# RWKV-6 attention and a gated feed-forward on one core: token pairs for the first four blocks, and the whole order of work changed

## The chip, the cores and the metric

The kernel runs on one NeuronCore of a Trainium2 chip. The core has five engines with queues of their own: TensorE (PE; its weight loads are listed as PEld), VectorE (DVE), ScalarE (ACT), GpSimd (POOL) and SyncE (SP), which issues most of the DMAs. Each engine takes its instructions in the order in which they were written and waits where an operand is not there yet. Sixteen DMA engines move data between HBM and the on-chip memory SBUF; TensorE writes to eight PSUM banks. The metric is the device time of one launch in microseconds (us); less is better.

## The reference

Inputs are r, k, v, w of shape (4 batches, 8 heads, 768 tokens, 48), u of (8, 48), and the weights of a feed-forward layer. First a recurrence over tokens, for every batch and head:

```python
for t in range(S):
    cur = np.einsum('bhd,bhe->bhde', u[None] * kt, vt)
    y[:, :, t] = np.einsum('bhd,bhde->bhe', rt, state + cur)
    state = wt[:, :, :, None] * state + np.einsum('bhd,bhe->bhde', kt, vt)
```

Then x, the rows of y with the heads side by side (3072 rows of 384), goes through:

```python
rms = np.sqrt(np.mean(x * x, axis=-1, keepdims=True) + 1e-06)
xn = x / rms * rms_g
g = xn @ w_gate                      # 384 -> 1536
silu = g * (1.0 / (1.0 + np.exp(-g)))
return (silu * (xn @ w_val) @ w_out) # 1536 -> 384
```

## The kernel before

**Blocks.** The 768 tokens of a batch are six chunks of 128. A block n.j is chunk n of batch j, 24 in all; its tokens lie on the 128 partitions, its 8 x 48 = 384 values on the free axis. Inside a block the recurrence becomes products. `ln` takes the logarithm of w, `cs_mm` sums it over tokens on TensorE with a triangular mask, `exp_r` and `exp_k` give decay factors, `r_mul` and `k_mul` apply them to r and k in bf16. `rk_pe` transposes the two on TensorE and `rk_tr` copies the result to SBUF (for chunks 2 to 5 `rk_tr` is a DMA transpose on SP instead). `q_mm` makes the scores of the even heads and of the odd heads in two PSUM banks, `q_mask_e`, `q_copy_o` and `q_mask_o` mask them, and `y_mm` multiplies them with v (`cast_v`, bf16) and adds the older state's part. `st_mm` and `st_new` carry the state to the next chunk. The term with u is apart: `bonus_mul` (r times k times u) and `bonus_v` on GpSimd, `bonus_sum` on VectorE; `x_add` on VectorE adds it to y.

**Feed-forward.** `x_sq`, `x_rstd`, `xn_mul` normalise; `xn_pe` and `xn_out` transpose and apply the gain (the last two chunks use a DMA transpose `xn_tr` and `xn_gain` on GpSimd). Four blocks make a group of 512 columns. For each group there are 12 `gate_mm` and 12 `val_mm` (one bank each, L617 or L622), `silu` on ScalarE, `h_mul` on VectorE, and four output products `o_mm` (12 matmuls each, L660) with `o_out` and `out_dma`. The groups follow the chunks, but the first holds blocks 0.0, 0.1, 1.0 and 1.1, and the second 0.2, 0.3, 1.2 and 1.3.

**Pairs of w.** For chunks 0 and 1 (set `WIN`) w is loaded for both chunks at once, with two neighbouring tokens on a partition, so that a DMA packet holds 2 x 48 fp32 = 384 bytes; r, k and v, and w of the other chunks, come in packets of 192. `cs_mm` then needs two products for each of its sums (L404, L411) and mask `mw`; elsewhere (`ONE_SUM`) it needs one (L419), and `cs_add` on VectorE makes the second sum from the first.

**What sets the order.** A table `ORDER` of some 1,050 steps, written out by hand, is walked from top to bottom; each step appends its instructions to the engines it uses. So the table fixes the order on every engine, the loads on SP and the four loads of gate and value weights on GpSimd (`load_gv`, L351) included. A number after a colon asks for fillers ahead of a step: matmuls with zeros (L238, L240) that keep TensorE running. Sets such as `CAST_ACT` or `K_POOL` choose the engine of a step. PSUM banks rotate in rings: two "a", two "b", four "q". SBUF tiles rotate too: eight tiles each for r, k and v (`NIN`), six for the transposed r and k (`NRKT`).

Of the kernel before, what the change touches and what calls it, by code (L numbers as in the profile page):

```python
# [9 lines left out]
FP32 = mybir.dt.float32  # L10
BF16 = mybir.dt.bfloat16
# [14 lines left out]
load_r.0.0 load_w.0.0 u_mm.0.0 ln.0.0 load_v.0.0 load_k.0.0 cs_mm.0.0:2 load_r.1.0 load_w.0.1 u_out.0.0 load_k.1.0  # L26
load_k.0.1 load_w.0.3 load_v.0.1 exp_r.0.0 exp_k.0.0 r_mul.0.0 cast_v.0.0 load_r.0.1 bonus_mul.0.0 load_k.1.1
bonus_sum.0.0 bonus_v.0.0 k_mul.0.0 cs_mm.1.0 load_r.1.1 load_v.1.1 load_v.1.0 load_w.0.2 rk_pe.0.0:2 rk_tr.0.0
exp_r.1.0 w_tot.1.0 w_tot.0.0 st_mm.0.0 r_mul.1.0 st_new.0.0 q_mm.0.0:4 load_k.0.3 load_r.0.3 load_r.0.2 load_k.0.2
load_v.0.2 ln.0.1 q_mask_o.0.0 exp_k.1.0 cs_mm.0.1 exp_r.0.1 k_mul.1.0 exp_k.0.1 rk_pe.1.0 load_v.0.3 rk_tr.1.0  # L30
bonus_mul.1.0 q_mask_e.0.0 load_k.1.3 load_r.1.2 load_k.1.2 load_r.1.3 load_v.1.2 bonus_mul.0.1 load_w.2.1 load_w.2.0
load_v.1.3 load_w.2.3 q_mm.1.0:2 cs_mm.1.1 exp_r.1.1 exp_k.1.1 r_mul.0.1 k_mul.0.1 w_tot.0.1 q_mask_o.1.0
bonus_sum.1.0 load_gv.0.1 cast_v.0.1 load_r.2.0 bonus_sum.0.1 r_mul.1.1 load_w.2.2 rk_pe.0.1:2 ln.0.3 y_mm.0.0
rk_tr.0.1 st_mm.0.1:4 x_add.0.0 q_mask_e.1.0 st_new.0.1 cs_mm.0.3:3 bonus_v.0.1 cast_v.1.0 q_mm.0.1:1 y_mm.1.0
k_mul.1.1 bonus_v.1.0 cast_v.1.1 q_copy_o.0.1 x_sq.0.0 bonus_mul.1.1 load_r.2.1 x_add.1.0 exp_r.0.3 load_r.2.2
x_sq.1.0 load_r.2.3 load_k.2.0 q_mask_e.0.1 w_tot.1.1 rk_pe.1.1:1 rk_tr.1.1 q_mm.1.1:7 q_mask_o.1.1 load_gv.0.0
q_mask_o.0.1 y_mm.0.1:8 g_mm.0.0 bonus_sum.1.1 ln.0.2 x_rstd.1.0 xn_mul.1.0 x_rstd.0.0 xn_mul.0.0 exp_k.0.3
bonus_v.1.1 load_gv.1.0 q_mask_e.1.1 x_add.0.1 x_sq.0.1 x_rstd.0.1 y_mm.1.1 x_add.1.1 k_mul.0.3 xn_pe.1.0:2 xn_pe.0.0
cs_mm.0.2 g_out.0.0 xn_out.1.0 x_sq.1.1 xn_mul.0.1 xn_out.0.0 r_mul.0.3 st_mm.1.1:3 x_rstd.1.1 st_mm.1.0 xn_mul.1.1
# [90 lines left out]
def kernel(  # L130
# [130 lines left out]
    def load_w(n, j):  # L261
# [4 lines left out]
        else:  # L266
            if ("w", n, j) not in inp:
                inp["w", n, j - j % 2] = inp["w", n, j - j % 2 + 1] = pin.tile([128, 2 * DM], FP32, name="wt", bufs=NIN // 2)
# [445 lines left out]
```

## Time and profile before

| | |
|---|---|
| time, median of three runs | 204.7 us (204.5 to 206.58) |
| the profiled execution | 203.96 us, its span 202.2 us |
| granted TensorE clock | 0.998 |
| busy: TensorE, VectorE, ScalarE, GpSimd | 95%, 78%, 67%, 62% of the span |
| DMA packets | 121,567, of which 116,420 under 512 bytes |
| first feed-forward matmul, end of the last matmul | 30.21 us, 199.0 us |

The span runs from the first instruction to the last. A busy TensorE includes fillers, and the matmul ends are modelled, so starts are the surer number. In rows of groups the last figures are the busy time, the mean ns of one, and the idle time of the engine before them with what ended it; in rows in order of time the first two figures are start and duration, and a bracket gives the idle time before the instruction.

### The profile page before, as it was taken

The numbers are of one execution on the slowest core, as the hardware profiler recorded it, in microseconds if no ns is written. First come the engines' busy times: TensorE is split into PE (matmuls) and PEld (weight loads), VectorE is DVE, ScalarE is ACT, GpSimd is POOL, SyncE is SP. The second block draws the span as 40 slices with busy tenths as digits, with TensorE's granted clock in tenths as the row PEclk, the third lists the DMA queues.
The fourth block names the chain that finished last, engine by engine and source line by source line (L and its number), as shares of the span: only waits on it lengthen the run. The fifth ranks groups of instructions, "written<-read, shape, count | busy, mean of one in ns | idle before, by whom it ended". The sixth has DMA issues, their size and how long they took to land.

```text
span 202.2 us, 4604 instructions
## 1 busy us (share of the span) xinstructions
PE 191.3 (95%) x1677; PEld 121.9 (60%) x1694; DVE 157.5 (78%) x307; ACT 135.0 (67%) x278; POOL 124.4 (62%) x178
## 2 busy tenths in 40 slices
PE   1999799999999999999999998999999999999993
PEld 0566485565568998865556664656555555555562
DVE  6489789799989799997999998988989782225711
ACT  2637885779699657898678985899676683335310
POOL 6488959175769962689858556988699554200000
PEclk9999999999999999999999999999999999999999
DMA  6999999999999998989899999995464013030132
GB/s 144 231 234 207 212 208 202 195 179 208 206 184 225 160 212 191 210 185 188 199 176 215 237 188 203 183 190 108 134 179 104 0 23 99 0 117 0 63 115 99
DMA packets 121567, 32.42 MB, mean 160 GB/s; under 512 B 116420, under 2 KB 120392, under 8 KB 121544
## 3 DMA queue, kind: packets, MB, share of 16 engines
q1 hardware_dynamic: 119504, 28.58, 66.6%
q0 software_dynamic: 2032, 3.54, 9.9%
q8 instruction: 13, 0.21, 0.4%
q14 instruction: 10, 0.08, 0.1%
q10 hardware_dynamic: 8, 0.00, 0.0%
HBM read 25.96 MB, written 4.72 MB: 152 GB/s over the span
## 4 chain that ended last, share of the span: by engine, by line
PE 65%; ACT 3%; DMA 2%; DVE 2%; issue 1%; SPq 0%; DVEq 0%; ACTq 0%
PE ps_av L617 7%; PE ps_bu L617 7%; PE ps_au L617 7%; PE ps_bv L617 6%; PE ps_qx L660 6%; PE ps_qv L660 6%; PE ps_qu L660 5%; PE ps_qz L660 4%; PE ps_au L622 2%; PE ps_bu L622 2%; DMA rkT<-rk 2%; PE ps_av L622 2%; PE ps_bv L622 2%; ACT L249 1%; PE ps_au L419 1%; PE ps_qv L500 1%
## 5 line engine op out<-in xcount | busy, mean ns | idle before, releaser
L660 PEld LDWEIGHTS <-ht 128*128 128x128 bf16 x300 | 28.1, 98 | 17.5 <-DVE ht L646 1.0
L251 ACT ACTIVATE sg<-ps_av 128x512 bf16<-128x512 f32 x36 | 21.5, 597 | 22.8 <-PE ps_av L617 18.0
L646 DVE TENSOR_TENSOR ht<-ps_bv,sg 128x512 bf16<-128x512 f32 x29 | 19.9, 687 | 13.9 <-PE ps_bv L617 12.9
L251 ACT ACTIVATE sg<-ps_au 128x512 bf16<-128x512 f32 x36 | 21.5, 596 | 11.5 <-PE ps_au L617 7.7
L617 PEld LDWEIGHTS <-wg_sb 128*128 128x128 bf16 x180 | 19.2, 114 | 15.9 <-issue 0.6
L617 PEld LDWEIGHTS <-wv_sb 128*128 128x128 bf16 x180 | 19.2, 114 | 15.7 <-issue 0.5
L465 POOL TENSOR_TENSOR ruk<-rt,kt 128x384 f32<-128x384 f32 x24 | 24.0, 1001 | 3.7 <-DMA kt<-in_k_dram 2.8
L475 POOL TENSOR_TENSOR ydiag<-vt,diag 128x384 f32<-128x384 f32 x24 | 20.4, 859 | 9.4 <-DVE diag L470 9.1
L617 PE MATMUL ps_av<-xnt,wg_sb 128*128 128x512 bf16 x88 | 25.0, 381 | 0.3
L466 POOL TENSOR_TENSOR ruk<-ruk,u_bc 128x384 f32<-128x384 f32 x24 | 24.0, 1001 | 1.9
L617 PE MATMUL ps_bu<-xnt,wv_sb 128*128 128x512 bf16 x86 | 24.8, 380 | 0.4
L646 DVE TENSOR_TENSOR ht<-ps_bu,sg 128x512 bf16<-128x512 f32 x31 | 21.3, 686 | 4.8 <-PE ps_bu L617 3.1
L617 PE MATMUL ps_au<-xnt,wg_sb 128*128 128x512 bf16 x87 | 23.6, 380 | 0.1
L617 PE MATMUL ps_bv<-xnt,wv_sb 128*128 128x512 bf16 x82 | 23.2, 380 | 0.2
L459 POOL TENSOR_TENSOR rk<-kt,ek 128x384 bf16<-128x384 f32 x16 | 15.9, 1001 | 9.7 <-ACT ek L251 5.9
L249 ACT ACT_TABLE_LOAD x14 | 18.0, 1283 | 1.9 <-PEq L698 1.6
L660 PE MATMUL ps_qx<-wo_sb,ht 128*128 128x384 bf16 x96 | 17.1, 326 | 0.2 <-DVE ht L646 0.2
L558 ACT ACTIVATE junk<-xb 128x384 bf16<-128x384 f32 x24 | 12.5, 522 | 6.3 <-DVE xb L553 6.2
L571 ACT ACTIVATE xn<-xb,rstd 128x384 bf16<-128x384 f32 x24 | 14.2, 609 | 0.6 <-POOL rstd L567 0.5
L470 DVE TENSOR_REDUCE diag<-ruk 128x8 f32<-128x384 f32 x24 | 13.1, 544 | 1.9 <-POOL ruk L466 1.9
L660 PE MATMUL ps_qv<-wo_sb,ht 128*128 128x384 bf16 (+1 forms) x84 | 13.8, 314 | 0.0
L251 ACT ACTIVATE lw<-wt 128x384 bf16<-128x384 f32 (+1 forms) x20 | 11.6, 583 | 2.8 <-DMA wt<-in_w_dram 2.7
(170 smaller groups left out, 408.2 us busy)
## 6 DMA issues: line engine op xcount, KB each, us to landing
rt<-in_r_dram SPq DMA_DIRECT2D x24, 192.0 KB, 4.0
vt<-in_v_dram SPq DMA_DIRECT2D x24, 192.0 KB, 3.9
kt<-in_k_dram SPq DMA_DIRECT2D x24, 192.0 KB, 3.9
out_dram<-ob SPq DMA_DIRECT2D x23, 192.0 KB, 2.2
wt<-in_w_dram SPq DMA_DIRECT2D x16, 192.0 KB, 3.7
wt<-in_w_dram SPq DMA_DIRECT2D x4, 384.0 KB, 4.3
wo_sb<-in_moe_w_out_dram POOLq DMA_DIRECT2D x3, 384.0 KB, 7.3
wg_sb<-in_moe_w_gate_dram POOLq DMA_DIRECT2D x1, 768.0 KB, 9.2
```

The lines of the kernel that those rows point to most:

```text
L249: nc.scalar.preload_act_table_set(table_name)
L251: return nc.scalar.activation(**kw).ins
L459: eng.tensor_tensor(out=rk[:, n % 2, j, 1, :, 0:D], in0=inp["k", n, j], in1=bank["cs_k", n, j][:, 0:DM].rearrange("p (h d) -> p h d", h=H) ...
L465: nc.gpsimd.tensor_tensor(out=ruk[n, j], in0=inp["r", n, j], in1=inp["k", n, j], op=ALU.mult)
L466: nc.gpsimd.tensor_tensor(out=ruk[n, j], in0=ruk[n, j], in1=u_bc, op=ALU.mult)
L470: nc.vector.tensor_reduce(out=diag[n, j].rearrange("p h o -> p (h o)"), in_=ruk[n, j], axis=mybir.AxisListType.X, op=ALU.add)
L475: nc.gpsimd.tensor_tensor(out=ydiag[n, j], in0=inp["v", n, j], in1=diag[n, j].to_broadcast([128, H, D]), op=ALU.mult)
L571: nc.scalar.activation(out=xn, in_=xb[n, j], func=AF.Copy, scale=rstd[n, j][:, 1:2])
L617: nc.tensor.matmul(ps, lhsT=units(ws, c, f), rhs=x[:, c, :], start=(c == 0), stop=(c == KC - 1))
L622: nc.tensor.matmul(ps[:, i * TS // 2:(i + 1) * TS // 2], lhsT=units(ws, c, f + i), rhs=x[:, c, cols], start=(i == 0 and c == 0), stop=(i = ...
L646: nc.vector.tensor_tensor(out=ht[n][:, f, :], in0=v, in1=sg, op=ALU.mult)
L660: nc.tensor.matmul(ps[:, cols], lhsT=ht[n][:, f, b * L:(b + 1) * L], rhs=wo_sb[:, f, cols], start=(f == 0), stop=(f == FC - 1))
```

## The change

- Blocks 0.0, 0.1, 1.0 and 1.1 (set `PAIR`) take r, k, v and w by token pairs: one load brings both chunks of a batch, and a partition holds tokens 2p and 2p+1. Chunk 0 is then the lower 64 partitions of both halves, chunk 1 the upper 64. "n" of such a block names the odd or even token in loads, products and transposes, and the chunk in `st_mm`, `y_mm` and after. So scores, state and y of one chunk need both halves: `q_mm` has 16 matmuls in place of 8 (each with 64 result rows), `st_mm` 8 in place of 4, `y_mm` 16 in place of 8 over heads.
- For these four blocks `x_add` is gone. A new step `yd_mm` adds the bonus term to y in PSUM, with two fp32 products of 64 rows and 384 columns; `x_sq` and `xn_mul` read the bank.
- w of batches 2 and 3, chunks 0 and 1, comes by single tokens: four loads of 192 KB for two of 384 KB, the short form of `cs_mm`, and a `cs_add` for each of the four blocks.
- Tiles of r, k, v and of transposed r and k are double: 5, 5, 4 and 3 of them. A tile is free when both its blocks are done.
- `ones_row`, which `u_mm` needs, is set right after the identity. `mw` and `mask_nle` are gone; masks for pairs (`mp`, `mask_p`) and an fp32 identity are new. GpSimd masks the odd heads of 0.0 and 0.1 by a product.
- `ORDER` is another table (1,058 steps), with other choices of engine. The filler instructions fall from 70 to 43.

The diff, cut to its core (of `ORDER` two lines):

```diff
-load_r.0.0 load_w.0.0 u_mm.0.0 ln.0.0 load_v.0.0 load_k.0.0 cs_mm.0.0:2 load_r.1.0 load_w.0.1 u_out.0.0 load_k.1.0
+load_w.0.0 u_mm.0.0:4 u_out.0.0 ln.0.0 load_r.0.0 load_k.0.0 load_r.0.1 load_w.0.1 bonus_mul.1.0 load_k.0.1
...
-    NIN, NRUK, NYD, NRKT, NE, NXB, NSG, NQT, NHT = 8, 3, 6, 6, 4, 4, 3, 3, 2
+    NIN, NRUK, NYD, NRKT, NE, NXB, NSG, NQT, NHT = 4, 3, 5, 3, 4, 3, 3, 4, 2
+    HL = L // 2
...
-    CAST_ACT = sel("00 01 02 03 20 21 30 31 33 40 43 53")
+    CAST_ACT = sel("00 01 10 11 13 20 30 32 33 42 50 52 53")
...
-    WIN = sel("00 01 02 03 10 11 12 13")
+    WIN = sel("00 01 10 11")
+    PAIR = sel("00 01 10 11")
...
+    YD_PE = sel("00 01 10 11")
...
-        inp[which, n, j] = pin.tile([128, H, D], FP32, name=which + "t", bufs=NIN)
+        if (n, j) in PAIR:
+            both = pin.tile([128, 2 * DM], FP32, name=which + "t", bufs=NIN + (which != "v")).rearrange("p (h x) -> p h x", h=H)
+            inp[which, 0, j], inp[which, 1, j] = both[:, :, 0:D], both[:, :, D:2 * D]
+            nc.sync.dma_start(out=both,
+                              in_=t[j, :, 0:2 * L, :].rearrange("h (p i) d -> p h (i d)", i=2))
+            return
...
+            if (n, c) in PAIR:
+                for i in range(NP):
+                    for a in range(2):
+                        for ps, d in ((qe, slice(0, D)), (qo, slice(PD, PD + D))):
+                            nc.tensor.matmul(ps[a * HL:(a + 1) * HL, i, :], lhsT=t[d, NP + i, a, n, :],
+                                             rhs=t[d, i, a].rearrange("p b x -> p (b x)"),
+                                             start=(i == 0), stop=(i == NP - 1))
+                continue
...
+    def yd_mm(n, j):
+        xb[n, j] = bank.pop(("y", n, j))
+        if (n, j) in PAIR:
+            rows = slice(n * HL, (n + 1) * HL)
+            for m in range(2):
+                nc.tensor.matmul(xb[n, j][m * HL:(m + 1) * HL], lhsT=ident32[rows, rows],
+                                 rhs=ydiag[m, j][rows].rearrange("p h d -> p (h d)"), start=False, stop=True)
+            return
```

**SP, from the start.** `rt`, `kt`, `vt`, `wt` are the tiles of r, k, v and w; a shape that ends in 96 is a pair load. Before:

```order
L259 DMA rt<-in_r_dram 128x8x48
L271 DMA wt<-in_w_dram 128x8x96
L259 DMA vt<-in_v_dram 128x8x48
L259 DMA kt<-in_k_dram 128x8x48
L259 DMA rt<-in_r_dram 128x8x48
L271 DMA wt<-in_w_dram 128x8x96
L259 DMA kt<-in_k_dram 128x8x48 x2
L271 DMA wt<-in_w_dram 128x8x96
L259 DMA vt<-in_v_dram 128x8x48
```

After:

```order
L284 DMA wt<-in_w_dram 128x8x96
L265 DMA rt<-in_r_dram 128x8x96
L265 DMA kt<-in_k_dram 128x8x96
L265 DMA rt<-in_r_dram 128x8x96
L284 DMA wt<-in_w_dram 128x8x96
L265 DMA kt<-in_k_dram 128x8x96
L265 DMA vt<-in_v_dram 128x8x96
L284 DMA wt<-in_w_dram 128x8x48
L265 DMA vt<-in_v_dram 128x8x96
```

w of batch 0 now comes first, the pair loads of r, k and v follow, and the second v load (batch 1) closes the four blocks with the ninth load.

**ScalarE, the casts of v in the front.** `ek`, `ps_a`, `ps_b` hold decay factors, `lw` the logarithm, `vb` the cast v, `rkT` the transposed r and k, `qts` the scores. Before, from the second exponent of block 1.0 on:

```order
L251 ACTIVATE ek<-ps_bv 128x384
L251 ACTIVATE ps_au<-ps_au 128x388
L251 ACTIVATE ps_bu<-ps_bu 128x384
L251 ACTIVATE ps_av<-ps_av 128x388
L251 ACTIVATE ek<-ps_bv 128x384
L387 CAST vb<-vt 128x384
L251 ACTIVATE lw<-wt 128x2x8x48
L491 COPY rkT<-ps_qv 128x1024
```

After, from the exponents of batch 1 on:

```order
L255 ACTIVATE ek<-ps_bv 128x384
L558 CAST qts<-ps_qu 128x512
L255 ACTIVATE ps_au<-ps_au 128x388
L255 ACTIVATE ps_av<-ps_av 128x388
L407 CAST vb<-vt 128x384 x4
L255 ACTIVATE lw<-wt 128x8x48 x2
L522 COPY rkT<-ps_qv 128x16x64
```

All four v casts of the first blocks now stand together, in the order 1.1, 1.0, 0.0, 0.1, ahead of two logarithms and of the copy of the transposes of block 1.1; before, two of the four were GpSimd's.

**GpSimd, where the gate and value weights are issued.** `ruk` is the bonus product, `ydiag` the bonus times v, `wg_sb` and `wv_sb` are the weights. Before, from the bonus product of block 1.1 on:

```order
L465 TENSOR_TENSOR ruk<-rt,kt 128x384
L466 TENSOR_TENSOR ruk<-ruk,u_bc 128x384
L351 DMA wg_sb_126<-in_moe_w_gate_dram 128x3x512
L518 AFFINE_SELECT qts<-qts 128x512
L475 TENSOR_TENSOR ydiag<-vt,diag 128x384
L351 DMA wg_sb_127<-in_moe_w_gate_dram 128x3x1024
L566 TENSOR_SCALAR rstd<-rstd 128x1
L567 TENSOR_TENSOR rstd<-rstd,mhalf 128x1
L351 DMA wv_sb_129<-in_moe_w_val_dram 128x3x1024
```

After:

```order
L371 DMA wg_sb_126<-in_moe_w_gate_dram 128x3x512
L371 DMA wv_sb_128<-in_moe_w_val_dram 128x3x512
L484 TENSOR_TENSOR ruk<-rt,kt 128x384
L485 TENSOR_TENSOR ruk<-ruk,u_bc 128x384
L552 TENSOR_TENSOR qts<-qts,mask_p 128x512
L494 TENSOR_TENSOR ydiag<-vt,diag 128x384
L371 DMA wg_sb_127<-in_moe_w_gate_dram 128x3x1024
L409 CAST vb<-vt 128x384
L484 TENSOR_TENSOR ruk<-rt,kt 128x384
L485 TENSOR_TENSOR ruk<-ruk,u_bc 128x384
L371 DMA wv_sb_129<-in_moe_w_val_dram 128x3x1024
```

The small value weights, which stood further up, now follow the small gate weights, and a whole bonus product with a cast has come between the two large loads.

345 lines of the change are left out of this document (196 added, 149 removed).

## The prediction

> **What bounds the kernel now.** I read the page's totals first, then a split of the span into stages, then TensorE's order of time, then who waited for whom.
>
> ```profile
> span 202.2 us, 4604 instructions
> PE 191.3 (95%) x1677; PEld 121.9 (60%) x1694; DVE 157.5 (78%) x307; ACT 135.0 (67%) x278; POOL 124.4 (62%) x178
> DMA  6999999999999998989899999995464013030132
> ```
> TensorE (PE) is busy in 95% of the span. The DMA row, in tenths of 40 slices, is full for nearly three quarters of it too, so either could be the limit; the mean does not say. The stages do. These rows give busy time (and instructions) of PE, weight load, VectorE, ScalarE and GpSimd, then the granted clock and the DMA share; the cuts are where the first feed-forward matmul starts and where the last one ends.
>
> ```profile
> 0.00:30.21 30.21, 24.25 (x284) 16.16 (x285) 22.14 (x51) 18.06 (x40) 21.78 (x38) 1.00 1.03 206
> 30.21:199.00 168.79, 167.02 (x1394) 105.72 (x1409) 135.04 (x256) 116.91 (x239) 102.63 (x141) 1.00 0.73 153
> 199.00:202.20 3.20, 0.00 (x0) 0.00 (x0) 0.36 (x1) 0.00 (x0) 0.00 (x0) 0.86 0.27 95
> ```
> From 30.21 to 199.00 TensorE is idle for 168.79 - 167.02 = 1.8 us only: this stage is bound by TensorE's own work, and the DMA, at 0.73 there, is not late. The 30.2 us before it are another matter: VectorE is busy for 22.1, GpSimd for 21.8, and TensorE for 24.3, of which much is filler.
>
> ```profile
> 20.48 1.30 PE L240 MATMUL ps_qz<-zero 128*128 128x384 bf16 x7
> 22.64 0.23 PE L500 MATMUL ps_qz<-rkT 48*128 48x128 bf16 x1 [0.85 <-DVE rkT L489]
> 22.64 0.23 PE L502 MATMUL ps_qx<-rkT 48*128 48x128 bf16 x1
> ...
> 29.40 0.81 PE L240 MATMUL ps_bv<-zero 128*128 128x384 bf16 x4
> 30.21 0.81 PE L617 MATMUL ps_bv<-xnt,wv_sb 128*128 128x512 bf16 x2
> ```
> L240 multiplies zeros to keep TensorE running; seven of them fill 1.30 us and the scores still wait 0.85 for a copy on VectorE. The front ends at 30.21, with the first L617. The waits of TensorE say that after the start little is lost:
>
> ```profile
> PE ps_qu L372 <- POOL ones_row L338: 4.2, 1, 4.2
> PE ps_qz L500 <- DVE rkT L489: 0.9, 1, 0.9
> PE ps_qu L500 <- DMA rkT<-rk: 0.6, 1, 0.6
> ```
> So the time is a sum of three: the front (30.2), TensorE's work after it with few gaps (168.8), and the end (3.2). The profiled execution took 203.96 us in all, 1.7 more than its span; the median of the three runs shown is 204.7, 0.7 above that. I make the sum for the profiled execution and add 0.7 at the end.
>
> **After the front.** The change takes work off TensorE here. The pair form of the cumulative sum (L404, L408, L411) gives way to a single-token form (L419, L422) for batches 2 and 3:
>
> ```profile
> 26.32 0.49 PE L404 MATMUL ps_av<-lw,mw 128*128 128x384 bf16 x2
> 27.17 0.65 PE L240 MATMUL ps_qx<-zero 128*128 128x384 bf16 x3
> ...
> 115.74 0.33 PE L419 MATMUL ps_au<-lw,mask_lt 128*128 128x384 bf16 x1
> 116.01 2.11 PE L660 MATMUL ps_qv<-wo_sb,ht 128*128 128x384 bf16 x12
> 117.95 0.33 PE L419 MATMUL ps_av<-lw,mask_lt 128*128 128x384 bf16 x1
> ```
> The long form takes 26.32 to 27.17 = 0.85 us, the short one 115.74 to 116.01 = 0.27. Four blocks change, of which only 1.2 and 1.3 come after the front (0.2 and 0.3 are summed ahead of it in both orders): 2 x 0.58 = 1.2 us less. A bf16 product of 384 columns streams in 0.16 us (twelve between 116.01 and 117.95). Two fillers of that size among the first feed-forward units go, 0.3 us, and the state matmuls of block 0.3, four of a quarter of the width, move into the front, 0.2 at most. Together 1.7 us. The rest of TensorE's list after the front is the same in number and shape: 144 gate and value units, 25 output products, the scores of blocks 2 to 5. VectorE gains four cs_add of an x_add's size (0.56, in a row below), two of them here, beside 135 us of work in 169: nothing. The order is new throughout. Before, it left waits of 1.8 us; I allow 0.3 more for the new one, since transposes on SP, output products and feed-forward units stand in the same pattern. Bounds: 1.8 less (no wait left) and some 3 more (below). So 168.8 - 1.7 + 0.3 = 167.4.
>
> **The end** has the same steps (two half outputs, a copy, a DMA): 3.2. The last copy moves from VectorE to ScalarE, within 0.2 either way.
>
> **The front** is where the change is meant to act, and I follow it in order of time. Loads first. These rows have the engine's idle time and what ended it in brackets:
>
> ```profile
> 5.42 0.84 ACT L251 ACTIVATE lw<-wt 128x768 bf16<-128x768 f32 x1 [2.50 <-DMA wt<-in_w_dram]
> 7.08 1.00 POOL L465 TENSOR_TENSOR ruk<-rt,kt 128x384 f32<-128x384 f32 x1 [2.84 <-DMA kt<-in_k_dram]
> ...
> 19.11 0.50 POOL L389 CAST vb<-vt 128x384 bf16<-128x384 f32 x1 [0.62 <-DMA vt<-in_v_dram]
> ```
> w of batch 0, second in the queue, has landed by 5.42, and v of block 1.0, thirteen loads later, by 19.11. Those thirteen are fifteen units of 192 KB: if a load costs by its bytes, 13.7 / 15 = 0.91 us a unit and a pair load 1.83; if it costs by its packets (1,024 in each), 1.05 for either. I take 1.4, near the middle, as no row is nearer to one end. After the change w of batch 0 is first, one load earlier (4.4), and r, k of batch 0 land by 7.2, k of batch 1 by 11.4, v of batch 0 by 12.8 and v of batch 1, with one single w between, by 15.1 (12.8 by packets, 18.1 by bytes). So the inputs of the first four blocks are there 4 us sooner than 19.1. What is late next are the engines.
>
> GpSimd is first. Its costs:
>
> ```profile
> L465 POOL TENSOR_TENSOR ruk<-rt,kt 128x384 f32<-128x384 f32 x24 | 24.0, 1001 | 3.7 <-DMA kt<-in_k_dram 2.8 <-DMA rt<-in_r_dram 0.8
> L475 POOL TENSOR_TENSOR ydiag<-vt,diag 128x384 f32<-128x384 f32 x24 | 20.4, 859 | 9.4 <-DVE diag L470 9.1 <-DVE wcol L449 0.3
> L518 POOL TENSOR_SCALAR_AFFINE_SELECT qts<-qts 128x512 bf16<-128x512 bf16 x14 | 8.8, 638 | 4.4 <-ACT qts L511 4.3
> L602 POOL TENSOR_TENSOR xnt<-xnt,gT 128x384 bf16<-128x384 bf16 x8 | 6.5, 825 | 3.3 <-DMA xnt<-xn 3.3
> ```
> Three bonus products (two instructions of 1.00 each) can start at 7.2 and end at 13.4. Behind them stand, in this order, one bonus times v (0.86), the new mask by multiplication of 512 bf16 columns, and the key product of block 1.1. The mask has no row; a mask by selection takes 0.64, a bf16 product of 384 columns 0.83, an fp32 one 1.00, so it lies between 0.64 and 1.33 and I take 1.1. Key product done: 13.4 + 0.9 + 1.1 + 1.0 = 16.4. Its transposes end on TensorE at 17.4 (six fillers stand ahead of them), and ScalarE copies them out; this copy and the chain at the front's end have these rows:
>
> ```profile
> 15.91 0.51 ACT L387 CAST vb<-vt 128x384 bf16<-128x384 f32 x1
> 17.06 1.01 ACT L491 COPY rkT<-ps_qv 128x1024 bf16<-128x1024 bf16 x1
> ...
> 25.92 0.56 DVE L553 TENSOR_TENSOR xb<-ps_qx,ydiag 128x384 f32<-128x384 f32 x1 [0.30 <-PE ps_qx L548]
> 26.57 0.52 ACT L558 ACTIVATE junk<-xb 128x384 bf16<-128x384 f32 x1 [0.30 <-DVE xb L553]
> ```
> The copy (17.06) takes 1.0, so the scores of block 0.1 start at 18.5. VectorE, which has lost four x_add (25.92) of 0.56, I put at the same place: the last mask for block 0.0 done by 18, an estimate. ScalarE's four v casts (15.91; 0.5 each) stand from 15.2, just behind v of batch 1.
>
> Three edits I cost at nothing. With ones_row first, the 4.2 us wait above goes, but w is there at 4.4 only, and the sums warm earlier (a saving below 1 us for each of two) end ahead of GpSimd's 13.4, which hides it. The double rings hold as many blocks as before or more, and their first reuse comes with the fifth double tile, after the front. The masks that VectorE and GpSimd set up at the start lie ahead of the first landing.
>
> Here an instruction enters that the kernel before did not have on this path: yd_mm adds the bonus to y on TensorE, as two fp32 products of 64 x 384 for each block, where VectorE's x_add did it in 0.56. The nearest rows:
>
> ```profile
> 4.16 1.64 PE L372 MATMUL ps_qu<-u_bc,ones_row 1*128 1x384 f32 x2 [4.16 <-POOL ones_row L338]
> 5.74 0.82 PE L240 MATMUL ps_au<-zero 128*128 128x384 bf16 x2
> ...
> 24.96 0.38 PE L379 MATMUL ps_qu<-i,g_row 3*128 3x3 f32 x2
> 25.27 0.34 PE L545 MATMUL ps_qx<-st,rkT 128*128 128x96 bf16 x4
> ```
> The fp32 product of u took 4.16 to 5.74 = 1.58 us for 384 columns, but cold: in the next row two bf16 products of that size took 0.82, where three take 0.65 later. The fp32 product of 3 columns took 0.31 in the warm part. So one costs between 0.31 and 1.58; halving the cold one gives 0.8, and I take 0.85, 1.7 for a block; the upper end, 1.58, would need a cold TensorE, which the rows at 18 us and later exclude. The Trainium skill (FP8 and Floating Point Precision, TensorE Precision Notes) counts four passes for true fp32; by that and a 0.163 us pass one product would be 0.65, an estimate, the front up to 1.0 shorter than what follows, the sum 203.5. The two recorded parts of the row of u do not settle it.
>
> From 18.5 TensorE has no pause: scores 0.3, yd 1.7, scores 0.4, y of block 1.0 0.6, yd 1.7, state 0.3, y 0.4, yd 1.7 (its bonus is done on GpSimd at 23.9, in time), y 0.6, a transpose and a state 0.4, yd 1.7: it ends at 28.4 with small gaps. Then the way from the square to the first unit: 26.57 to 30.21 before, 3.6 with another block's scaling (0.6) between, which now lies earlier: 3.0. First feed-forward unit at 31.4, **1.2 us later** than 30.2. Fillers fall from 70 instructions to 43 and cost nothing either way, since they stood where TensorE waited.
>
> The gate and value weights are the last check, since GpSimd issues them:
>
> ```profile
> 25.35 0.80 POOL L351 DMA_DIRECT2D wg_sb<-in_moe_w_gate_dram  x1
> 27.36 0.85 POOL L351 DMA_DIRECT2D wv_sb<-in_moe_w_val_dram  x1
> ...
> wg_sb<-in_moe_w_gate_dram POOLq DMA_DIRECT2D x1, 768.0 KB, 9.2
> wv_sb<-in_moe_w_val_dram POOLq DMA_DIRECT2D x1, 768.0 KB, 11.5
> ```
> Before, the two large ones left at 25.35 and 27.36 and landed 9.2 and 11.5 us later. After, GpSimd's list puts them at 23.9 and 27.3, so they land at 33.1 and 38.8. TensorE wants them as its 7th and 12th unit, at 35.7 and 39.6: they are hidden, by 0.8 us for the second.
>
> **Sum:** 31.4 + 167.4 + 3.2 = 202.0 span, 203.7 with the 1.7 around it, 0.2 under the profiled execution. With 0.7 for the median: **204.5 us**, no change. A measurement of this kernel can tell a change of about 1% (2 us) from none, so the lines are 202.7 and 206.7.
>
> **Rivals.** *Faster: the halves of yd_mm run together and pair loads cost by packets.* The score matmuls L500 and L502 above, on other partitions, start in the same 0.01 us, so TensorE can overlap small products. The halves read the same 64 partitions and write to different ones. Then a block's yd is 0.85, and GpSimd's start, 0.8 sooner with k at 6.4, becomes the bound: yd of block 0.1 starts at 23.1, the front ends at 28.9. TensorE would then want the second value weights at 37.1 and wait until about 37.5 to 38. Time 204.5 - 2.5 + 0.4 = 202.4. The Trainium skill (TensorEngine Tiling (Array Packing), Key Properties) states that different tiles load and multiply in parallel, which is this rival's first half; no row here shows two products on the same rows doing it. Against it: the two parts of u's product (x2) took their time one after the other. *Slower: ScalarE is held at the v casts.* The changed list has all four casts in one place, with v of batch 1 first; behind them stand two logarithms and the copy of the transposes of block 1.1. It decides from v landing later than 15.2. By bytes it lands at 18.1, all behind it is 2.9 late, and the front ends at 34.3: 207.4. For it: DMA share 1.03 in the front. Against: eleven of the thirteen loads behind 0.91 and 1.05 were single ones, so the pair's price by bytes, 1.83, is twice theirs only if a packet costs nothing of its own. *Not the change it says:* if pair loads save nothing and nothing waits for them, the time is the forecast's.
>
> Unpriced beside these: scores of block 5.0 follow the sums of block 5.0 by 8.5 us of TensorE work, 11.4 before; if SP holds its transposes as it did for block 4 (the 0.6 wait above), up to 2.4 us are lost. It goes into the upper end.
>
> **Chances:** forecast 0.47, faster rival 0.24, slower 0.29; the line of 1% divides them the same way, as the faster rival's 202.4 and the slower's 207.4 lie just past it. Range: 201.5 (faster rival with the weights in time, and no wait left after the front) to 208.0 (slower rival and part of the loss at block 5).
>
> **What would show it.** First feed-forward unit at 31.4 in the order of time (forecast), 28.9 or 34.3 (rivals); yd_mm at 0.85 an instruction, one behind the other; ScalarE's idle time before the casts, ended by v's DMA, near zero or 3 us; TensorE's idle time between front and end, 1.8 to 2.1; TensorE's wait at the scores of block 5.0. The prediction is wrong if the new order leaves gaps at many places after the front, which the list of instructions cannot show.

## The result and the profile after

The changed kernel took 216.07 us (median of 4; 214.11 to 217.49), the kernel before 205.64 beside it: ratio 1.047, with a 95% interval of 1.034 to 1.060. The ratio leaves out executions more than 1.5% above the fastest of their kernel, which is why it is not the quotient of the two medians. The forecast was 204.5, its range ended at 208.0. The profiled execution took 216.56 us with a span of 214.8, against a forecast span of 202.0.

The totals of the page of the changed kernel, with its rows of 40 slices for the granted clock and the DMA:

```profile
span 214.8 us, 4689 instructions
PE 198.8 (93%) x1735; PEld 124.7 (58%) x1735; DVE 156.5 (73%) x309; ACT 137.9 (64%) x285; POOL 122.9 (57%) x172
PEclk9999859999999997999999999999999999999999
DMA  6999999999758597495998999989835203301112
```

TensorE's share of the span has fallen only from 95 to 93%, which would hide the case: it is busy for longer (198.8 us against 191.3) and has 12.6 us more of span. Two things are new in the other rows. The granted clock dips in slices 5 and 6 (21 to 32 us) and in slice 16 (81 to 86 us), where it was full throughout before; and the DMA, which ran full until about 136 us, has holes between 54 and 102 us, in a kernel whose loads are still to come.

The same three stages as before, cut at the first feed-forward matmul and at the last matmul's end, and three short windows (busy time of TensorE, weight load, VectorE, ScalarE, GpSimd; granted clock; DMA share; GB/s):

```profile
0.00:32.68 32.68, 29.85 (x345) 18.77 (x346) 22.33 (x53) 20.72 (x47) 23.52 (x36) 0.90 1.05 222
32.68:211.58 178.90, 168.91 (x1393) 105.89 (x1390) 134.13 (x257) 116.87 (x238) 99.41 (x136) 0.99 0.68 139
211.58:214.80 3.22, 0.00 (x0) 0.00 (x0) 0.00 (x0) 0.32 (x1) 0.00 (x0) 1.00 0.25 92
25.01:31.85 6.84, 6.84 (x62) 4.41 (x61) 2.69 (x6) 4.26 (x14) 2.98 (x4) 0.50 1.18 216
79.30:82.75 3.45, 0.19 (x10) 0.02 (x4) 0.65 (x1) 1.05 (x3) 0.00 (x0) 1.00 0.81 161
83.04:86.45 3.41, 3.41 (x31) 2.59 (x28) 1.89 (x3) 0.59 (x1) 3.02 (x6) 0.50 0.76 155
```

The front ends 1.3 us later than forecast, the stage after it is 11.5 longer (178.9 against 167.4), the end is as forecast. TensorE is idle for 178.90 - 168.91 = 10.0 us after the front, where it was 1.8. And it runs at half the clock twice: for 6.84 us in the front, and for 3.41 us just behind a gap of 3.45 us.

TensorE's waits name that gap and the next ones:

```profile
PE ps_qx L540 <- DMA rkT<-rk: 3.3, 1, 3.3
PE ps_au L686 <- DVE rk L472: 1.8, 1, 1.8
PE ps_qz L540 <- DMA rkT<-rk: 1.1, 1, 1.1
PE ps_qu L244 <- DVE half_of L325: 1.0, 1, 1.0
PE ps_av L441 <- ACT lw L255: 1.0, 1, 1.0
```

The first lies between the scores of block 2.2 and those of block 2.3, which wait for a transpose by DMA. (The fourth, for half_of, is at the very start.) The changed kernel's SP queue, from whose list the transposes, loads and outputs leave in order, shows how it came about:

```profile
72.29 0.56 SPq L749 DMA_DIRECT2D out_dram<-ob  x1
72.90 0.46 SPq L272 DMA_DIRECT2D vt<-in_v_dram  x1
73.46 5.71 SPq L518 DMA_TRANSPOSE rkT<-rk  x1
79.23 0.57 SPq L272 DMA_DIRECT2D vt<-in_v_dram  x1
```

An output of 192 KB (block 0.0) leaves at 72.29, a load behind it, and then one transpose, that of block 2.3, takes 5.71 us to issue. All loads of chunk 3 but the first stand behind it. What the DMA moved is seen in two windows of 1 us, the first in this stretch, the second at the next output of this kind (columns as above):

```profile
77.50:78.50 1.00, 1.00 (x12) 1.00 (x10) 1.00 (x3) 0.28 (x1) 1.00 (x2) 1.00 0.44 52
...
87.50:88.50 1.00, 1.00 (x18) 0.71 (x15) 1.00 (x2) 0.99 (x3) 0.95 (x1) 1.00 0.13 49
```

In the second, the DMA share is 0.13: two of 16 engines, moving 49 GB/s, and all that moves is the output. It is the output of a paired block. Its rows hold every second token in the kernel's layout, and so the change writes it in this form (a paired block's 128 rows as 2 x 64):

```
if (i, j) in PAIR:
    dst = dst.rearrange("(x a) m -> a x m", a=2)
nc.sync.dma_start(out=dst, in_=bank.pop(ob)[:, cols])
```

Counted from the trace's DMA records, packets of 1536 B (one row of the output) that start in half a microsecond, the two lower kernels being runs told below:

```
kernel                      form      half us from   starts   ns each
before                      128           75.5          83        66
after                       2 x 64        78.0          16        65
before, outputs 2 x 64      2 x 64        81.0          16        65
before, outputs 8 x 16      8 x 16        66.5          60        70
```

16 x 65 ns in 500 ns is 2.1 engines at work (60 x 70 ns is 8.4). At that rate the 128 rows of an output take 4.2 us. From the first row's start to the last row's end the four outputs of paired blocks took 4.6 to 5.5 us, where the same four of the kernel before took 1.0 to 1.6. What is queued behind such an output on these two engines waits as long. The load of v issued at 72.90 shows it: of its 1,024 packets of 192 B, 896 (fourteen sixteenths) start between 74.0 and 75.5 us, and the last 128 (two sixteenths) only from 79.0 on, when the output's last row is out (78.96).

### The profile page after: what moved, and what is told of

The parts are those of the page before. It is cut to its first block, busy times and chain, and to the rows that moved or that the text cites. A ratio compares the mean times of both kernels' runs of the same rounds, so it can differ in the third digit from the quotient of the medians.

```text
span 214.8 us, 4689 instructions
## 1 busy us (share of the span) xinstructions
PE 198.8 (93%) x1735; PEld 124.7 (58%) x1735; DVE 156.5 (73%) x309; ACT 137.9 (64%) x285; POOL 122.9 (57%) x172
## 4 chain that ended last, share of the span: by engine, by line
PE 54%; DMA 16%; POOL 12%; ACT 6%; DVE 5%; SPq 3%; issue 3%; POOLq 0%; DVEq 0%
PE ps_bu L686 6%; PE ps_au L686 6%; PE ps_av L686 6%; DMA kt<-in_k_dram 5%; PE ps_bv L686 5%; DMA wo_sb<-in_moe_w_out_dram 5%; PE ps_qx L729 5%; PE ps_qu L729 4%; DMA wt<-in_w_dram 3%; PE ps_qv L729 3%; DMA rkT<-rk 2%; POOL ruk L485 2%; POOL ydiag L494 2%; POOL ruk L484 2%; PE ps_qz L729 2%
## 5 line engine op out<-in xcount | busy, mean ns | idle before, releaser
L686 PE MATMUL ps_au<-xnt,wg_sb 128*128 128x512 bf16 x90 | 24.4, 380 | 2.4 <-DVE rk L472 1.8
L686 PE MATMUL ps_bu<-xnt,wv_sb 128*128 128x512 bf16 x93 | 25.3, 381 | 0.6 <-ACT ek L255 0.6
L485 POOL TENSOR_TENSOR ruk<-ruk,u_bc 128x384 f32<-128x384 f32 x24 | 24.6, 1025 | 1.9
L494 POOL TENSOR_TENSOR ydiag<-vt,diag 128x384 f32<-128x384 f32 x24 | 19.8, 831 | 7.9 <-PE ps_qx L729 5.4
L686 PE MATMUL ps_av<-xnt,wg_sb 128*128 128x512 bf16 x90 | 24.3, 379 | 0.0
L478 POOL TENSOR_TENSOR rk<-kt,ek 128x384 bf16<-128x384 f32 x15 | 14.9, 999 | 12.7 <-ACT ek L255 11.0
L729 PE MATMUL ps_qu<-wo_sb,ht 128*128 128x384 bf16 (+1 forms) x96 | 16.1, 316 | 0.3 <-DMA wo_sb<-in_moe_w_out_dram 0.3
L567 POOL TENSOR_SCALAR_AFFINE_SELECT qts<-qts 128x512 bf16<-128x512 bf16 x12 | 7.6, 638 | 14.1 <-ACT qts L558 14.1
L640 ACT ACTIVATE xn<-xb,rstd 128x384 bf16<-128x384 f32 x20 | 11.9, 607 | 1.5 <-POOL rstd L636 1.5
```

The costliest lines, as they stand in the source:

```text
L478: eng.tensor_tensor(out=rk[:, n % 2, j, 1, :, 0:D], in0=inp["k", n, j], in1=bank["cs_k", n, j][:, 0:DM].rearrange("p (h d) -> p h d", h=H) ...
L485: nc.gpsimd.tensor_tensor(out=ruk[n, j], in0=ruk[n, j], in1=u_bc, op=ALU.mult)
L494: nc.gpsimd.tensor_tensor(out=ydiag[n, j], in0=inp["v", n, j], in1=diag[n, j].to_broadcast([128, H, D]), op=ALU.mult)
L567: nc.gpsimd.affine_select(out=qts[n, j][:, 1], in_=qts[n, j][:, 1], compare_op=ALU.is_gt, fill=0.0, base=0, pattern=[[0, NP], [1, 128]], c ...
L640: nc.scalar.activation(out=xn, in_=xb[n, j], func=AF.Copy, scale=rstd[n, j][:, 1:2])
L686: nc.tensor.matmul(ps, lhsT=units(ws, c, f), rhs=x[:, c, :], start=(c == 0), stop=(c == KC - 1))
```

## Experiments: the output and the clock

Two causes could be seen, the slow output and the half clock, and two rivals for the wait at 79 us: that SP's list puts the transposes of chunk 2 ahead of the loads of chunk 3, and that the rings of double tiles release too late.

**Outputs in halves.** The form alone is undone: each paired block's output in two DMAs of 64 rows.

```
-        nc.sync.dma_start(out=dst, in_=bank.pop(ob)[:, cols])
+        for a in range(2):
+            nc.sync.dma_start(out=dst.rearrange("(x a) m -> a x m", a=2)[a],
+                              in_=src[a * HL:(a + 1) * HL])
```

> The changed kernel, but the output of each of the four paired blocks leaves in two DMAs of 64 rows, where it left in one of 2 x 64 rows. Theory (output): in the changed kernel's trace the packets of 1536 B of such an output start 16 in half a microsecond and take 65 ns each, which is about two DMA engines at work, so an output lasts 4 to 5 us and holds the loads and transposes behind it. In halves it should last under 1.5 us. Then TensorE's wait of 3.3 us at the scores of block 2.2, the half clock behind it (1.7 us lost) and most of the waits at 90 to 116 us go: 5 to 9 us, a median of 207 to 211. Rival (order on SP): the transposes of chunk 2 stand ahead of the loads of chunk 3 and wait for GpSimd; the outputs' form does nothing, and the median stays at 215 to 217 with the wait of 3.3 us in place. Rival (rings of double tiles): the same 215 to 217.

Measured: 206.68 us, just below the 207 to 211 that was expected, ratio to before 1.013 (1.006 to 1.020). The same place in its SP queue:

```profile
71.23 1.18 SPq L750 DMA_DIRECT2D out_dram<-ob  x2
72.46 0.58 SPq L272 DMA_DIRECT2D vt<-in_v_dram  x1
73.14 1.36 SPq L518 DMA_TRANSPOSE rkT<-rk  x1
74.55 0.58 SPq L272 DMA_DIRECT2D vt<-in_v_dram  x1
```

The transpose issues in 1.36 us in place of 5.71. The windows of this kernel:

```profile
0.00:32.27 32.27, 29.51 (x345) 18.05 (x346) 22.23 (x53) 20.00 (x47) 22.98 (x36) 0.89 1.05 224
32.27:201.11 168.84, 165.79 (x1378) 105.20 (x1390) 134.38 (x257) 117.62 (x238) 99.88 (x137) 1.00 0.70 147
```

The stage after the front falls from 178.9 to 168.8, with the order on SP and the rings untouched: neither rival is needed for these 10 us. The front, and its half clock (0.89 in the mean), stay.

**The same form in the kernel before.**

```
-        nc.sync.dma_start(out=out[row0:row0 + L, cols], in_=...)
+        dst = out[row0:row0 + L, cols]
+        if i < 2 and j < 2:
+            dst = dst.rearrange("(x a) m -> a x m", a=2)
+        nc.sync.dma_start(out=dst, in_=...)
```

> The kernel before, with nothing changed but the output DMA of the four blocks that the change pairs, which is given the form 2 x 64 rows (every second row). These rows of the output come in another order; nothing else is left out or changed. Theory (output): each of these four DMAs lasts 4 to 5 us instead of about 2 and holds the transposes and loads behind it, so the kernel before is slowed by 2 to 8 us, to 207 to 213. Rivals (order on SP, rings): its order and rings are as they were, so it stays at 204 to 206.

Measured: 213.97 us, ratio 1.051 (1.045 to 1.057), 1 us above the range. A window with one such output by itself, and the stage after the front, which was 168.79:

```profile
80.50:81.50 1.00, 1.00 (x20) 0.77 (x18) 0.96 (x3) 0.00 (x0) 1.00 (x3) 1.00 0.13 51
...
29.48:208.99 179.51, 171.36 (x1393) 106.39 (x1409) 135.55 (x256) 116.89 (x239) 102.76 (x141) 0.98 0.72 145
```

Four DMAs in another form, with the order, the rings and every other instruction as before, lose 10.7 us in that stage. Part of that is the clock: it halved for two windows of 3.41 us (from 94.0 and from 100.8) behind the gaps.

**Eight groups in place of two**, in the kernel before (a=8).

> The kernel before, with the output DMA of the same four blocks in the form 8 x 16 rows (every eighth row) instead of 2 x 64; these rows of the output come in another order, nothing is left out. Theory (the count of the outer dimension sets how many DMA engines share an output): at 8 the packets run on eight engines, an output lasts about 1 us, and the time is within 1% of the kernel before, 203.5 to 206. Rival (it is the permuted rows, every row on its own in memory, that make the output slow): as slow as with 2 x 64, 212 to 215.

Measured: 204.41 us, ratio 0.993 (0.990 to 0.997), beside a kernel before at 205.96. So it is not rows that are apart in memory that cost the time; it is the size of the outer dimension, and at 8 there is no loss left to measure (60 starts in half a microsecond, in the table above).

**Fillers in the front.** The changed kernel, its outputs as they were, with eight more products of zeros:

```
- q_mm.0.1    st_mm.0.1    y_mm.0.1    y_mm.1.1
+ q_mm.0.1:2  st_mm.0.1:3  y_mm.0.1:2  y_mm.1.1:1
```

> The changed kernel with eight more filler products in the front: two ahead of the scores of block 0.1, three ahead of the state of block 0.1, two ahead of y of block 0.1, one ahead of y of block 1.1 (1.3 us of TensorE work where it waited 0.5, 0.5 and 0.4). Theory (clock): the granted clock of 0.5 from 25.0 to 31.9 us comes from TensorE's waits just before it; with the fillers the clock stays at 1.0, and the first feed-forward unit comes at 30.5 to 31.5 in place of 32.7; median 213.5 to 215. Rival (GpSimd sets the front): the clock is at 1.0 but the first unit stays within 0.5 of 32.7. Second rival: the clock falls all the same, because the fp32 products use a quarter of the array; then nothing moves.

Measured: 212.27 us, ratio 1.042 (1.035 to 1.049). Its front:

```profile
0.00:30.10 30.10, 27.80 (x353) 16.87 (x354) 22.14 (x53) 19.64 (x46) 22.60 (x36) 1.00 1.05 224
30.10:206.68 176.58, 167.28 (x1378) 105.70 (x1390) 134.24 (x257) 118.05 (x239) 100.33 (x137) 0.99 0.71 144
```

More work on TensorE ends the front 2.6 us sooner, at a clock of 1.00 in place of 0.90. The first unit came at 30.1, sooner than the 30.5 to 31.5 that I expected, and the time is 1.2 us below the range for it.

**Both.**

> The changed kernel with the two edits together: outputs of paired blocks in two halves, and the eight fillers. If the output and the clock are the two main losses, the gains add: 5 to 9 and 1 to 2.5 us, a median of 205 to 210. If the order on SP or the rings are the main loss, it stays at 213.5 or above.

Measured: 204.44 us, ratio 1.000 (0.997 to 1.004), a little below the range that was expected. Its windows:

```profile
0.00:30.12 30.12, 27.38 (x354) 16.52 (x354) 22.06 (x53) 19.63 (x46) 22.60 (x36) 1.00 1.04 224
30.12:199.23 169.11, 165.97 (x1378) 105.13 (x1390) 134.28 (x257) 118.10 (x239) 100.28 (x137) 1.00 0.73 150
199.23:202.30 3.07, 0.00 (x1) 0.00 (x0) 0.00 (x0) 0.32 (x1) 0.00 (x0) 1.00 0.27 96
```

With the two losses taken out, what is left of the change costs nothing and brings nothing. In one table (us, of the profiled executions; the last column is the forecast):

| stage | before | after | halves | fillers | both | forecast |
|---|---|---|---|---|---|---|
| front | 30.21 | 32.68 | 32.27 | 30.10 | 30.12 | 31.4 |
| after the front | 168.79 | 178.90 | 168.84 | 176.58 | 169.11 | 167.4 |
| end | 3.20 | 3.22 | 3.09 | 3.22 | 3.07 | 3.2 |
| span | 202.2 | 214.8 | 204.2 | 209.9 | 202.3 | 202.0 |

The output is worth 10.6 us of span without the fillers and 7.6 with them, the fillers 4.9 with the slow output and 1.9 without it: the two don't simply add, perhaps because the length of the front decides which loads meet a slow output; no run shows that by itself.

**The kernel before without 15 of its fillers** (q_mm.1.1:7 and y_mm.0.1:8 lose their numbers).

> The kernel before, without the seven filler products ahead of the scores of block 1.1 and the eight ahead of y of block 0.1 (2.4 us of TensorE work where it would wait anyway); all else as it is. Theory (clock): without them TensorE idles for some 2 to 3 us between 20 and 24.5, the granted clock halves for 3.4 to 6.8 us from about 24, and the time rises by 1 to 3 us, to 205.5 to 207.5. Rival (fillers stand where TensorE waits and cost or bring nothing, as the prediction put it): 204 to 205, the granted clock 1.0.

Measured: 207.26 us, within the 205.5 to 207.5 that was expected, beside a kernel before at 205.96; ratio 1.008 (1.004 to 1.012). The clock halved here too, and the front ended at 32.53 in place of 30.21:

```profile
23.37:30.20 6.83, 5.46 (x51) 4.18 (x52) 4.66 (x10) 5.43 (x15) 4.39 (x7) 0.50 1.13 192
```

So the fillers of the kernel before were worth about 1.7 us of time (0.8%, by the ratio), though they stand where TensorE waits.

## Experiments: what the clock counts

In all profiles so far the clock changed on a grid of 3.41 us (the slow stretches last 3.41, 6.83 or 10.24), but TensorE's busy share of a window does not say which will be followed by half the clock. The two runs here change only the shape of the added fillers, on the kernel with halved outputs. The times in the first expectation are those of the kernel with slow outputs, by a slip; its outputs are in halves, so that its time is to be held against 204.4 (clock held) and 206.7 (clock halved). The first run changes all eight added fillers, the second six of them.

```
- lhsT=zero, rhs=bc_mid(zero, 3)            # 128 rows x 128 columns
+ lhsT=zero[:, 0:32], rhs=bc_mid(zero, 3)   # first run: 32 columns
+ lhsT=zero[0:32], rhs=bc_mid(zero[0:32], 3)  # second run: 32 rows
```

> The changed kernel with the same eight added fillers as in the second run (212.3), of the same number and length (384 columns each), but with 32 columns of weights in place of 128, so that each uses a quarter of the array. Theory (the clock is granted by how much of the array works, not by how long TensorE is busy): over the runs so far, windows of 3.41 us with a product of rows, columns and streamed columns below 0.36 of the full array are followed by half the clock, windows above 0.40 are not, while the busy share does not divide them; with a quarter of the array the eight fillers add 0.01 each in place of 0.05, the clock falls to 0.5 between 23 and 32 us, and the time is that of the changed kernel, 214.5 to 217. Rival (busy time counts): clock 1.0 in the front, first unit at 30.1, 211.5 to 213.5.

Measured: 204.52 us, ratio 1.002 (1.000 to 1.005), first unit at 30.15: the clock held, and the theory, that the worked area of the array counts, fell.

> The changed kernel with halved outputs and eight added fillers (204.4), where six of the eight (at the state of block 0.1, y of block 0.1, y of block 1.1) have 32 rows of weights and of moving data in place of 128: same count and length, a quarter of the rows. In the profiles so far a window of 3.41 us in which the streamed columns, each product weighted by its share of the 128 rows, come to under 0.42 of the clocks is followed by half the clock, and above 0.45 not; with columns of weights in the place of rows this does not hold, since fillers of 32 columns held the clock. Theory (rows count): the window that begins at 19 to 23 us falls to about 0.37 to 0.43, the clock halves, first unit at 31.5 to 32.5, median 206 to 207.5. Rival (any product counts for its time): clock 1.0, first unit at 30.1, median 204 to 205.

Measured: 208.47 us, ratio 1.019 (1.013 to 1.026); the clock halved, for three windows, and the first unit came at 34.5, later than the 31.5 to 32.5 that was expected; the time is 1 us above its range. Of the run with narrow fillers and of the run with short ones, the fillers (rows * columns of the weights) and a window that decides:

```profile
21.97 0.65 PE L244 MATMUL ps_qz<-zero 128*32 128x384 bf16 x3 [0.30 <-ACT xn L643]
...
18.96:22.37 3.41, 3.09 (x49) 1.49 (x42) 2.33 (x4) 3.27 (x10) 3.31 (x4) 1.00 1.19 197
22.37:25.79 3.42, 3.42 (x54) 1.93 (x53) 2.33 (x5) 1.99 (x8) 3.34 (x6) 1.00 1.23 207
```

```profile
22.05 0.64 PE L244 MATMUL ps_qz<-zero 32*128 32x384 bf16 x3 [0.31 <-ACT xn L643]
...
19.94:23.35 3.41, 3.10 (x52) 1.67 (x43) 2.53 (x4) 3.25 (x12) 3.33 (x5) 1.00 1.19 191
23.35:33.59 10.24, 10.24 (x87) 5.88 (x85) 4.05 (x9) 4.83 (x14) 4.22 (x7) 0.50 1.17 211
```

TensorE is busy for 3.09 us of 3.41 in the one and for 3.10 in the other; the first is followed by a full clock, the second by half. The two windows don't begin at the same point of the work, but that does not decide: in all ten executions with narrow fillers the mean clock was 0.998 to 1.0, in all four with short ones 0.975 to 0.983. A measure that divides them: the columns streamed by all products that start in a window (an fp32 record counted twice), each weighted with its rows over 128, as a share of what 3.41 us could stream at 2.4 columns a nanosecond (384 in 0.16 us):

```
kernel, window from (us)       TensorE busy   share by rows   clock after
after, 21.6                        0.81           0.34            0.5
halves, 20.1                       0.81           0.42            0.5
before, outputs 2 x 64, 97.4       0.41           0.36            0.5
short fillers, 19.9                0.91           0.40            0.5
fillers, 74.3                      0.56           0.45            1.0
before, outputs 8 x 16, 21.8       0.69           0.49            1.0
narrow fillers, 19.0               0.91           0.61            1.0
before, 20.4                       0.75           0.67            1.0
```

Over all profiles, of windows at the full clock behind the start, none from 0.45 on is followed by half the clock and none up to 0.42 by the full one. The measure was found in the earlier profiles and foretold the run with short fillers (expected 0.37 to 0.43, found 0.40), so it was tested once; for windows that are already slow it does not divide the cases.

## Experiments: what is left of the front

**x_add in place of yd_mm**, on the kernel with both edits (YD_PE empty, each yd_mm in the order an x_add). In this kernel the bonus is added in the wrong half rows, since the sum in two halves on TensorE was also what sorted them.

> The changed kernel with halved outputs and fillers (204.4), but the bonus of the four paired blocks added by VectorE (x_add, 0.56 us each, at the same places of the order) and not by the fp32 products on TensorE. Theory (the two halves of the fp32 product run together, 0.65 us a block, in a front that GpSimd sets): TensorE is spared 2.6 us, VectorE has 2.2 more, and the chain to the first unit gets no shorter; first unit at 29.6 to 30.6, median 203.8 to 205. Rival (as the prediction had it: the products cost the front 1.2 us or more): first unit at 29.0 or sooner and median 203.5 or less. Rival (VectorE is then late): first unit at 31 or later, 205.2 or more.

Measured: 207.07 us, ratio 1.006 (1.002 to 1.010), where the kernel with yd_mm had 1.000 (0.997 to 1.004). The second rival is right. At the places where the order has yd_mm, VectorE now stands and waits for TensorE's y (L606), and what follows in its list is late: the state of block 0.1 (L588) comes at 26.11, where it came at 23.71 with yd_mm, and TensorE waits 2.6 us for it. In the profiled execution, which took 209.05 us:

```profile
21.03 0.56 DVE L622 TENSOR_TENSOR xb<-ps_qz,ydiag 128x384 f32<-128x384 f32 x1 [1.22 <-PE ps_qz L606]
...
23.90 0.56 DVE L622 TENSOR_TENSOR xb<-ps_qz,ydiag 128x384 f32<-128x384 f32 x1 [0.66 <-PE ps_qz L606]
...
26.11 0.54 DVE L588 TENSOR_TENSOR st<-ps_qx,wcol 128x384 bf16<-128x384 f32 x1
...
PE ps_qv L601 <- DVE st L588: 2.6, 1, 2.6
```

The clock then halved in all ten executions (its mean is 0.973 to 0.992), which the rival did not name. Whether this wait brought it down or the TensorE work that is gone with yd_mm, no run separates.

**GpSimd relieved:**

```
- x_rstd.0.0 load_gv.0.0 ... load_gv.0.1 bonus_mul.0.1 bonus_sum.0.1 q_mask_o.0.1
+ x_rstd.0.0 bonus_mul.0.1 load_gv.0.0 ... load_gv.0.1 bonus_sum.0.1
- ODD_DVE = sel("10 ...")
+ ODD_DVE = sel("01 10 ...")
```

> The changed kernel with halved outputs and fillers (as in the run with both edits, 204.4), and on top of it GpSimd relieved in the front: the bonus product of block 0.1 ahead of the first two weight DMAs, and the odd mask of block 0.1 taken from GpSimd's 1.17 us to VectorE, straight from the scores, without ScalarE's copy. Theory (GpSimd sets the front): in that run GpSimd works without a break from 6.8 to 27.4 us and the bonus of block 0.1 is done at 23.3, TensorE's product with it starts at 24.0; now the bonus comes 1 us or more sooner, and the first feed-forward unit moves from 30.1 to 29.2 to 29.7: median 203.4 to 204.0. Rival (TensorE's own work and ScalarE's chain of squares set the front): the first unit stays within 0.2 of 30.1, median 204.2 to 204.8, or worse if the weights, issued 2 us later, are late.

Measured: 205.41 us beside 205.96 for the kernel before, ratio 0.997 (0.993 to 1.000). The bonus of block 0.1 was done at 22.28 in place of 23.37, but the first unit moved from 30.12 to 30.01 only: GpSimd did not set the front; the rival was right.

**TensorE's own list**, on top of it: two fillers fewer ahead of the state of block 0.1, and VectorE's first bonus sum behind the products of block 0.0.

```
- w_tot.1.0 bonus_sum.1.0 w_tot.0.0 r_mul.0.0 k_mul.0.0    st_mm.0.1:3
+ w_tot.1.0 w_tot.0.0 r_mul.0.0 k_mul.0.0 bonus_sum.1.0    st_mm.0.1:1
```

> The kernel with halved outputs, fillers and the bonus product moved ahead (205.4 against 206.0 of the kernel before on the same chip), with two more edits in the front: VectorE takes the sum of the first bonus behind the two products of block 0.0 (it stood ahead of them and waited 0.35 for GpSimd, and TensorE waited 0.7 there), and one filler ahead of the state of block 0.1 in place of three, since there the three ran after the wait was over. Theory (TensorE's own order sets the front now): the first unit moves from 30.0 to 29.2 to 29.7 and the time to 0.99 to 0.995 of the kernel before. Rival (GpSimd sets it): the first unit stays at 30.0, ratio 0.995 to 1.0. Rival (clock): with two fillers fewer the clock halves, the first unit comes at 31 or later, ratio above 1.003.

Measured: 203.43 us, ratio 0.997 (0.995 to 1.000). The first unit came at 29.28, as the theory had it, with the clock held, but the ratio is no better than that of the run before it, and short of the 0.99 to 0.995 expected: the span fell by 0.3 only (202.0 to 201.7), as TensorE, now earlier, waits 0.4 for the gate weights:

```profile
34.18 0.84 PE L686 MATMUL ps_av<-xnt,wg_sb 128*128 128x512 bf16 x3 [0.40 <-DMA wg_sb<-in_moe_w_gate_dram]
```

**The large weights sooner**, on top of that (load_gv.1.0 ahead of bonus_v.0.1, load_gv.1.1 ahead of bonus_mul.0.3):

> The kernel of the front-order run (203.4 against 204.1 of the kernel before), with the two large weight DMAs issued ahead of the bonus times v of block 0.1 and of the bonus product of block 0.3, since TensorE waited 0.4 for the gate weights there. Theory: that wait goes and nothing takes its place, the span falls by 0.3 to 0.6, ratio to the kernel before 0.994 to 0.997. Rival: the product of the bonus of block 0.1 is later by 0.5 and takes it back, ratio 0.997 to 1.0.

Measured: 203.01 us, ratio 0.995 (0.992 to 0.998), in the range that the theory gave. The wait for the weights went; the profiled span did not fall with it (201.8 against 201.7, its front being 0.6 longer), so that the mechanism is not shown, and with intervals that overlap neither is a gain over the run before. By its ratio this is the fastest version: 0.5% below the kernel before, 5% below the changed one. The gain that pairs were to bring is spent before it reaches the first feed-forward unit: the casts of v for the first four blocks stood at 14.85 in the changed kernel without a wait, where one of them still waited until 19.11 before.

## Why the prediction was wrong

**A step that is not in it: the output of a paired block.** The prediction went through the loads, the casts, the products and the weights, and for "the end" through the last outputs, but never priced the four outputs whose form the change alters (2 x 64 rows). That is most of the miss: 10.6 us of span by undoing it, 10.7 in the stage after the front by putting it into the kernel before. In the sum it stands in the term after the front, 168.8 - 1.7 + 0.3: the 0.3 us allowed for new waits came out at 8.2 (TensorE's idle time went from 1.8 to 10.0), and TensorE's busy time rose by 1.9 in place of falling by 1.7. The loads whose shape changes were priced, the outputs were not. The Trainium skill (DMA: Bandwidth & Descriptors, "Why a DMA increments its semaphore by 16 and not by 1") says that a DMA is split over the largest number of engines, up to 16, that divides the slowest dimension of both sides. By that, 2 x 64 gives two engines and 8 x 16 eight, and the trace agrees: a DMA share of 0.13, and 16 against 60 starts in half a microsecond.

**"Fillers fall from 70 instructions to 43 and cost nothing either way, since they stood where TensorE waited."** This step failed. They hold the clock. Without enough of them it halved for 6.84 us in the front: eight fillers brought 2.2 us by the medians with halved outputs (206.68 to 204.44), and taking 15 out of the kernel before cost 1.7 (0.8%). The Trainium skill (TensorE: Matmul & The Clock Gate, Part 1) has the window of 3413 ns and a gate that goes by how busy the array was; the lengths of 3.41, 6.83 and 10.24 agree, the busy share alone does not.

**"From 18.5 TensorE has no pause"** failed with it. The changed kernel's rows of that stretch (idle time in brackets):

```profile
14.85 1.75 ACT L407 CAST vb<-vt 128x384 bf16<-128x384 f32 x4
15.36 1.01 POOL L478 TENSOR_TENSOR rk<-kt,ek 128x384 bf16<-128x384 f32 x1
17.80 1.01 ACT L522 COPY rkT<-ps_qv 128x1024 bf16<-128x1024 bf16 x1 [0.38 <-PE ps_qv L501]
19.09 0.84 PE L615 MATMUL ps_qz<-ydiag,ident 64*64 64x384 f32 x4
22.29 0.50 PE L581 MATMUL ps_qz<-vb,rk 64*128 64x96 bf16 x8 [0.30 <-ACT xn L640]
23.74 0.86 PE L615 MATMUL ps_qv<-ydiag,ident 64*64 64x384 f32 x4 [0.22 <-POOL ydiag L494]
26.31 1.55 PE L615 MATMUL ps_qu<-ydiag,ident 64*64 64x384 f32 x4
```

yd_mm was put at 1.7 us a block, two products of 0.85 one behind the other. It took 0.65 from its start at 19.09 to the next product (0.84 with its end): one product takes 0.65 and the halves run together, the first part of the faster rival. TensorE then had pauses, and the fewer products it had, the nearer it came to the lower clock; the last yd_mm (26.31) runs at half speed. With the clock held the front ended at 30.1, so the forecast of 31.4 was 1.3 too long and the rival's 28.9 about as much too short. The four blocks of yd_mm are 2.6 us in place of 6.8; of these 4.2 us the pauses, and the fillers that hold the clock, took back some 2.9.

**What was right in the front.** The key product of block 1.1 was done at 16.37 (forecast 16.4), the copy began at 17.80 and the scores of 0.1 started at 18.87 (18.5). The casts stood at 14.85 with no wait, so v had landed in time and the slower rival's mechanism did not happen; the time came out slower for other reasons. In the trace's DMA records, by the starts of packets of 384 B, a pair load follows the last one every 1.2 us (the 1,024th packet at 3.72, the 5,120th at 8.60), which is nearer to the price by packets (1.05) than to that by bytes (1.83); 1.4 had been taken. The large weights landed at 32.7 and 37.3 (33.1 and 38.8), hidden.

**After the front**, with the two losses taken out: TensorE's work fell from 167.0 to 166.0, by 1.0 and not by 1.7; its idle time rose from 1.8 to 3.1, by 1.4 and not by 0.3. So 169.1 against 167.4. The two errors, 1.3 in the front and 1.7 here, nearly cancel, and the span of that kernel, 202.3, agrees with the forecast's 202.0 in part by luck. The wait that was left unpriced, at the scores of block 5.0, did not come: behind 120 us TensorE's one wait above 0.15 us in the changed kernel is 0.61, at 161.82, for a normalised block.

The prediction named "gaps at many places after the front" as what would make it wrong. They came, but from the outputs and not from the order. The double rings and the place of ones_row showed no cost in any run here.

## What to carry to other kernels

When a change alters a layout, price every DMA that touches it, the last output too: look at its outer dimension, and at the DMA share while it is alone (0.13 is two engines of 16). Zero products that stand in a wait were not free to remove here: they held the clock, and a busy TensorE with weights of few rows did not hold it. When two losses are found, undo each alone and both together; here 10.6 and 4.9 gave 12.5.

## What the runs showed of the hardware that was not expected

- A DMA of 192 KB in the form 2 x 64 moved 49 to 51 GB/s on two engines; in the form 8 x 16 it did no harm. Behind such an output a transpose took 5.71 us to issue, against 1.36.
- The clock follows a window of 3.41 us, and fillers with weights of 32 rows did not hold it where fillers with weights of 32 columns did, at the same busy time (3.10 and 3.09 us of 3.41).
- Two fp32 products on one set of 64 rows, writing to two sets of 64 columns, take 0.65 us together at the full clock: their four recorded parts start in two pairs, 0.3 to 0.4 us apart.
